# Attention units followed by their transposes one unit later, weight decoding in smaller steps, an earlier load of x

## The chip, the core and the metric

One NeuronCore of a Trainium2 chip runs the kernel. The metric is the device time of one execution in microseconds (us). Engines: TensorE (PE, its weight loads PEld), VectorE (DVE), ScalarE (ACT), GpSimd (POOL), and SyncE (SP), which issues most of the transfers.

## The reference

Inputs are float32 q, k, v of shape 4 x 8 x 768 x 64 (batch, heads, positions, width), a 64 x 6 projection, and float64 weights of a feed-forward block. What is computed, cut to its core:

```python
q_bits = (einsum('bhsd,dk->bhsk', q, proj) > 0)        # six sign bits per position; k_bits alike
mask   = q_bucket[:, :, :, None] == k_bucket[:, :, None, :]
scores = where(mask, (q @ k.T) / 8, -1e9)
attn   = exp(scores - max); attn /= attn.sum(-1) + 1e-9
x      = (attn @ v), heads side by side                 # 4 x 768 x 512
h      = relu(x @ w_in)                                  # 512 -> 1024
conv   = three taps along the positions, per channel of h
out    = (h * sigmoid(conv)) @ w_out                     # 1024 -> 512
```

## The kernel before

**Attention.** Two heads of a batch are a pair; there are 16 pairs (`pi` 0 to 15). A pair has 12 units (`Unit`), one for 128 queries of one head, so there are 192 units. One loop over `i` (L452) writes the program, and the order of its calls is the order of the instructions on every engine; no scheduler moves anything. Step `i` issues for unit `u = units[i]` the four score products (`products`, L276, PE, tile s in PSUM), the row maximum with the copy to SBUF (`maximum`, L284, DVE, tile e), the exponential (L291, ACT) and, for the unit before, the sum's end and its reciprocal (L295, L298, DVE) and the scaling (`normalise`, L299, POOL). For unit `w = units[i - LAG]` it issues six transposes (`transposes`, L304, PE, tile t in PSUM) and their copy (`to_sbuf`, L311, ACT, tile at). After every fourth `w` the product with v follows one step later (`values`, L319, 24 matmuls, called V below), and at the step after that its copy out of PSUM (L324, DVE, tile x) and a store to DRAM (xd, L325).

Three PSUM buffers under the tag "S" are taken in turn by s, t and the pair's hash. So the transposes of step `i` take the buffer that the scores of unit `i - 1` leave free, once DVE has done the maximum of unit `i - 1`. The value products and later the hidden layer take turns in two buffers under the tag "M". e has `EB` buffers.

**The next pair.** In steps k = 1 to 7 of each pair, `prepare` splits the next pair's q and k, tile R, into a high and a low part (L194 and L199 on POOL, for each of two heads), computes the hash (L209, L212, L214), and moves the parts by transfers of SP's queue. R has one buffer: its next load (L181) waits for those transfers.

**Weights.** 16 blocks of 128 x 512 float64 weights are fetched (L164, one each six steps) and decoded to two float32 parts. A block takes four DVE instructions (L94, L96, L101, L103), two on ACT (L86, L135) and three on POOL (L89, L138, L139). `split_weights` is a generator; from step `DECODE` on, every second step takes one piece of it:

```python
if i >= DECODE and i % 2 == 0:
    next(weights_todo, None)
```

**x of batch 0** is loaded from DRAM at the start of pair `X0` (L371, four transfers) and split on POOL by one instruction each third step (L379, L381).

**Feed-forward.** At `i == n` (192) `feed_forward` starts. Each of its steps has 12 matmuls of the hidden layer (L342, tile h under the tag "M"), Relu and first tap on ACT (L347, L349), two taps on DVE (L351), Sigmoid on ACT (L354), a product on DVE (L355), a split (L360 ACT, L361 POOL), and the output product (L391). Its first steps are interleaved with the last units' transposes.

Of the kernel before, what the change touches and what calls it, by code (L numbers as in the profile page):

```python
# [7 lines left out]
F32 = mybir.dt.float32  # L8
F32R = mybir.dt.float32r
# [3 lines left out]
ALU = mybir.AluOpType  # L13
# [4 lines left out]
P = 128  # L18
# [9 lines left out]
MASKED = -8.0e9  # L28
F32_MAX = 2.0 ** 127 * (2.0 - 2.0 ** -23)
F64_MIN = 2.0 ** -15  # L30
LAG, EB = 3, 5
FLAG = 3
BURST = 4
PREP = 1
PREP_N = 6
DECODE = 14
FETCH = 6
X0 = 8
WC = 512


# [1 line left out]
def lsh_attention_conv_ffn(ctx, tc, qk, v, hw, w_in, conv_w, w_out, consts, ident_in, out):  # L43
    nc = tc.nc
    PSUM = bass.MemoryType.PSUM
    cp = ctx.enter_context(tc.tile_pool(name="const", bufs=1))
# [19 lines left out]
    weights = {}  # L66
# [6 lines left out]
    class Decode:  # L73
# [17 lines left out]
        def upper(self):  # L91

            V, up, low = nc.vector, self.up, self.low
            V.tensor_scalar(low, low, 3, 0x3FFFFFFF, ALU.logical_shift_left, ALU.bitwise_and)  # L94
            yield
            V.scalar_tensor_tensor(up, self.hi, -0x40000000, low, ALU.bitwise_and, ALU.bitwise_or)  # L96
            yield

        def lower(self):
            V, up, low = nc.vector, self.up, self.low  # L100
            V.tensor_scalar(low, up, -0x800000, None, ALU.bitwise_and)  # L101
            yield
            V.scalar_tensor_tensor(self.lowf, self.lo, 2.0 ** -52, self.lowf, ALU.mult, ALU.mult)  # L103
            yield

    def split_weights():

        todo, ends = [], None

        def ahead():
            if fetched:
                raw, name = fetched.pop(0)
                todo.append(Decode(raw, WC, name))
                todo[-1].size()

        ahead()
        ahead()  # L120
        yield
        for d in todo:
            d.clamp()
        yield
        while todo:
            d = todo.pop(0)
            ahead()
            yield from d.upper()
            if ends:
                ends()  # L130
            if len(todo) == 2:
                todo[-1].clamp()
            yield from d.lower()
            blk = weights[d.name] = cp.tile([P, 2, WC], F32R, tag=f"w{d.name}", name=f"w{d.name}")
            nc.scalar.copy(blk[:, 0, :], d.upf)  # L135

            def ends(d=d, blk=blk):
                nc.gpsimd.tensor_tensor(d.upf, d.upf, blk[:, 0, :].bitcast(F32), ALU.subtract)  # L138
                nc.gpsimd.tensor_tensor(blk[:, 1, :], d.upf, d.lowf, ALU.add)  # L139

        ends()

    def decode_taps(raw):
        d = Decode(raw, NFC * 3, "cw")
        d.size()
        yield
        d.clamp()
        yield
        yield from d.upper()
        yield from d.lower()  # L150
        nc.vector.tensor_tensor(cw.rearrange("p f k -> p (f k)"), d.upf, d.lowf, ALU.add)


# [2 lines left out]
    blocks += [(w_out[f * P:(f + 1) * P], f"o{f}") for f in range(NFC)]  # L156
    fetched, taps = [], []
    weights_todo = split_weights()

    def fetch(n):  # L160
# [287 lines left out]
    next(first)  # L448
    pairs[1].load()
    n, tail, x0 = len(units), None, None  # L450
    outs, av, splits = [], None, iter(())
    for i in range(n + LAG + 1):  # L452
        u = units[i] if i < n else None
        w = units[i - LAG] if LAG <= i < n + LAG else None
        prev = units[i - 1] if 1 <= i <= n else None
        pi, k = divmod(i, 2 * NCK)
        burst = w and w.tq == QB // P - 1 and w.h == 1
        if u:
            u.products()
            u.maximum(prev)  # L460
        elif prev:
            prev.total()
        for o in outs:
            o()
        outs = []
        if w:
            w.transposes()
            w.to_sbuf()
        if u:
            u.exponential()  # L470
        if prev:
            prev.normalise()
        if i in (0, 2):
            next(first, None)
        if u and k == PREP and pi + 1 < len(pairs):
            prep[0] = pairs[pi + 1].prepare()
        next(prep[0], None)
        if av:
            outs.append(values(*av))
            av = None  # L480
        if burst:
            av = w.pair, w.qb, w.pair.at
        if u and k == PREP + PREP_N and pi + 1 < len(pairs):
            pairs[pi + 1].load_v()
            if pi + 2 < len(pairs):
                pairs[pi + 2].load()
        if i == 3:
            taps.append(decode_taps(cwr))
        for g in taps:
            next(g, None)  # L490
        if i % FETCH == FETCH - 1:
            fetch(1)
        if i >= DECODE and i % 2 == 0:
            next(weights_todo, None)
        if pi == X0 and k == 0:
            x0 = load_x(0)
            splits = split_x(x0)
        if x0 and k % 3 == 2:
            next(splits, None)
        if i == n:  # L500
            tail = feed_forward(x0)
        if tail:
            next(tail)
# [47 lines left out]
```

## Time and profile before

| | |
|---|---|
| time, median of 3 runs | 767.1 us (765.78 to 767.71) |
| the profiled execution's own time | 765.89 us |
| its span (first to last instruction) | 764.1 us, mean granted clock 0.985 |
| PE busy | 711.3 us (93%) |
| DVE busy | 489.6 us (64%) |
| ACT busy | 486.2 us (64%) |
| POOL busy | 448.4 us (59%) |
| attention | from 7 to about 477 us |
| feed-forward | from about 477 us to the end |

Read the table with care for stages: in the feed-forward part PE has matmuls without a break, so what the change is worth is read from the attention part and from the place where the two meet. Times of DMA and engines overlap; a wait counts only where PE stands behind it.

### The profile page before, as it was taken

How to read it: one execution, taken by the hardware profiler on the slowest of the kernel's cores; microseconds unless marked ns; L12 is line 12 of the kernel's file. 1: busy time of each engine (PE TensorE's matmuls, PEld its weight loads, DVE VectorE, ACT ScalarE, POOL GpSimd, SP SyncE). 2: the span in 40 equal slices, each digit the busy share in tenths (PEclk: the TensorE clock that was granted, in tenths of full speed). 3: DMA queues.
4: the chain of work that ended last, by engine and by line, in shares of the span. 5: the costliest groups of instructions: out<-in, count | busy, mean ns of one | idle time of the engine just before them, and what ended most of it. 6: DMA issues, size and time to landing. Idle time of an engine off the chain costs nothing.

```text
span 764.1 us, 13725 instructions
## 1 busy us (share of the span) xinstructions
PE 711.3 (93%) x4552; PEld 579.4 (76%) x4552; DVE 489.6 (64%) x1303; ACT 486.2 (64%) x892; POOL 448.4 (59%) x422
## 2 busy tenths in 40 slices
PE   5999888899898888989999999889999999999997
PEld 3767666667677666677777777778989899899986
DVE  7656776676667657666666655357666756665553
ACT  5777767677677756777777777535454545545453
POOL 5775776877867779878766553145326524642222
PEclk8999999999999989999999999999999999999999
DMA  3767556557566744653655640201210121101011
GB/s 110 185 182 202 157 172 178 156 169 212 131 186 180 215 133 108 177 146 83 175 146 131 185 104 15 90 7 42 80 45 1 42 84 41 42 1 42 0 42 42
DMA packets 39575, 84.79 MB, mean 111 GB/s; under 512 B 6960, under 2 KB 14672, under 8 KB 39504
## 3 DMA queue, kind: packets, MB, share of 16 engines
q1 hardware_dynamic: 36912, 75.47, 35.8%
q10 hardware_dynamic: 2592, 8.44, 3.3%
q8 instruction: 37, 0.61, 0.3%
q14 instruction: 34, 0.28, 0.1%
HBM read 33.70 MB, written 12.58 MB: 61 GB/s over the span
## 4 chain that ended last, share of the span: by engine, by line
PE 66%; DVE 19%; DMA 5%; POOL 4%; issue 3%; ACT 2%; SPq 1%; DVEq 0%; POOLq 0%; ACTq 0%
PE o L391 17%; PE h L342 17%; PE v L319 15%; DVE e L284 10%; PE s L276 8%; PE t L304 7%; DMA R<-in_qk 3%; POOL e L299 2%; DMA k<-R 2%; DVE wli L103 1%; DVE wlo L103 1%; PE hash L209 1%; DVE st L298 1%; DVE st L288 1%; DVE st L295 1%
## 5 line engine op out<-in xcount | busy, mean ns | idle before, releaser
L284 DVE TENSOR_SCALAR_CACHE_REDUCE e<-s 128x768 f32<-128x768 f32 x192 | 182.9, 953 | 137.4 <-PE s L276 120.5
L299 POOL TENSOR_SCALAR e<-e,st 128x768 f32<-128x768 f32 x192 | 186.1, 971 | 114.8 <-DVE st L298 98.5
L311 ACT COPY at<-t 128x768 f32<-128x768 f32 x192 | 151.8, 791 | 103.7 <-PE t L304 103.5
L291 ACT ACTIVATE e<-e,st 128x768 f32<-128x768 f32 x192 | 180.4, 940 | 25.2 <-DVE st L298 21.5
L304 PE MATMUL t<-ident,e 128*128 128x128 f32 x1152 | 162.9, 278 | 33.4 <-DVE st L295 26.5
L304 PEld LDWEIGHTS t<-ident,e 128*128 128x128 f32 x1152 | 131.0, 142 | 62.1 <-POOL e L299 52.1
L361 POOL TENSOR_TENSOR g<-ht,g 128x384 fp32r<-128x384 f32 x64 | 69.7, 1088 | 170.5 <-ACT g L360 138.2
L351 DVE SCALAR_TENSOR_TENSOR ht<-ht,cw 128x384 f32<-128x384 f32 (+1 forms) x128 | 119.2, 931 | 73.6 <-ACT ht L349 71.0
L342 PE MATMUL h<-x,wi 128*128 128x386 f32 x768 | 147.7, 341 | 2.7 <-DVE x L324 2.7
L342 PEld LDWEIGHTS h<-x,wi 128*128 128x128 f32 x768 | 138.0, 190 | 8.9 <-DVE x L324 3.1
L391 PE MATMUL o<-wo,g 128*128 128x512 f32 x576 | 143.6, 394 | 0.0
L319 PE MATMUL v<-at,v 128*64 128x256 f32 x1152 | 137.8, 387 | 2.1 <-ACT at L311 2.1
L391 PEld LDWEIGHTS o<-wo,g 128*128 128x128 f32 x576 | 107.2, 188 | 20.5
L319 PEld LDWEIGHTS v<-at,v 128*64 128x64 f32 x1152 | 79.5, 138 | 52.9 <-issue 15.9
L276 PE MATMUL s<-K,Q 128*128 128x384 f32 x384 | 116.3, 384 | 1.5 <-POOL K L243 1.2
L276 PE MATMUL s<-k,q 96*128 96x384 f32 x384 | 99.8, 341 | 2.3 <-DVE e L284 2.1
L354 ACT ACTIVATE ht<-ht 128x384 f32<-128x384 f32 x64 | 33.6, 525 | 96.9 <-DVE ht L351 96.9
L276 PEld LDWEIGHTS s<-K,Q 128*128 128x128 f32 x384 | 58.6, 192 | 21.8 <-issue 18.9
L276 PEld LDWEIGHTS s<-k,q 96*128 96x128 f32 x384 | 70.9, 191 | 3.1 <-ACT q L256 3.1
L355 DVE TENSOR_TENSOR ht<-ht 128x384 f32<-128x384 f32 x64 | 47.5, 741 | 33.7 <-ACT ht L354 33.7
L347 ACT ACTIVATE ht<-h 128x386 f32<-128x386 f32 x64 | 31.6, 494 | 37.3 <-PE h L342 37.1
L199 POOL TENSOR_TENSOR R<-R,hi 128x768 fp32r<-128x768 f32 x30 | 54.8, 1828 | 0.0
(65 smaller groups left out, 512.2 us busy)
## 6 DMA issues: line engine op xcount, KB each, us to landing
R<-in_qk SPq DMA_DIRECT2D x15, 768.0 KB
K<-hi SPq DMA_DIRECT2D x60, 192.0 KB
v<-in_v SPq DMA_DIRECT2D x16, 384.0 KB
xd<-x SPq DMA_DIRECT2D x48, 128.0 KB
x<-xd SPq DMA_DIRECT2D x16, 384.0 KB
out<-osb SPq DMA_DIRECT2D x24, 256.0 KB
Q<-hi SPq DMA_DIRECT2D x30, 192.0 KB
q<-hi SPq DMA_DIRECT2D x30, 192.0 KB
```

The costliest lines, as they stand in the source:

```text
L199: nc.gpsimd.tensor_tensor(lo, R, hi.bitcast(F32), ALU.subtract)
L276: nc.tensor.matmul(self.sp[:, half, :HS], A[:, h, qs], C[:, h, half * HS:(half + 1) * HS], start=(kk == 0), stop=(kk == 1))
L284: nc.vector.tensor_scalar(self.e.rearrange("p (a b) -> p a b", a=2), self.sp[:, :, :HS], MASKED, None, ALU.max, ALU.max, accum_out=self.st ...
L291: nc.scalar.activation(self.e, self.e, AF.Exp, bias=self.st[:, 1:2], scale=SCALE, accum_out=self.st[:, 2:3])
L299: nc.gpsimd.tensor_scalar(self.e, self.e, self.st[:, 3:4], 0.0, ALU.mult, ALU.add)
L304: nc.tensor.transpose(self.tp[:, c // 3, c % 3 * P:(c % 3 + 1) * P], self.e[:, c * P:(c + 1) * P], ident)
L311: nc.scalar.copy(pr.at[self.h][:, :, :, self.tq * P:(self.tq + 1) * P], self.tp[:, :, :3 * P].rearrange("p j (c q) -> p j c q", c=3))
L319: nc.tensor.matmul(av[h * D:(h + 1) * D, :QB], pr.v[:, c, h, :], ats[h][:, c // 3, c % 3, :], start=(c == 0), stop=(c == NCK - 1), tile_po ...
L342: nc.tensor.matmul(hp[:, :HW], w, x[:, c0:c0 + HW], start=(n == 0), stop=(n == 3 * NCC - 1))
L351: nc.vector.scalar_tensor_tensor(t[:, a:z], ht[:, o + k - 1 + a:o + k - 1 + z], cw[:, f, k:k + 1], t[:, a:z], ALU.mult, ALU.add)
L361: nc.gpsimd.tensor_tensor(g[:, 1, :], t, g[:, 0, :].bitcast(F32), ALU.subtract)
L391: nc.tensor.matmul(op, l, r, start=(f == 0 and i == 0), stop=(f == NFC - 1 and i == 2))
```

## The change

Four things change. `LAG` goes from 3 to 4 and `EB` from 5 to 6: the transposes of a unit come four steps after its products, and e has six buffers. The decoding of a weight block is cut into eight pieces instead of four (a DVE instruction in every other one, the POOL instructions in pieces of their own), it starts at step 10 instead of 14, and three of four steps take a piece (`RATE` 0.75) instead of every second one. x of batch 0 is loaded at the start of pair 6 (the seventh) and split from pair 9 on, instead of both from pair 8 on. The last pair's last V is followed at once by its copy. The number of instructions on each engine stays as it was.

```diff
-LAG, EB = 3, 5
+LAG, EB = 4, 6
-DECODE = 14
+DECODE, RATE = 10, 0.75
-X0 = 8
+X0, X0_SPLIT = 6, 9
...
     def split_weights():
-        todo, ends = [], None
+        todo, ends = [], iter(())
...
+        def finish(d, blk):
+            nc.gpsimd.tensor_tensor(d.upf, d.upf, blk[:, 0, :].bitcast(F32), ALU.subtract)
+            yield
+            nc.gpsimd.tensor_tensor(blk[:, 1, :], d.upf, d.lowf, ALU.add)
+
-        ahead()
         ahead()
         yield
-        for d in todo:
-            d.clamp()
+        todo[-1].clamp()
         yield
         while todo:
             d = todo.pop(0)
-            ahead()
-            yield from d.upper()
-            if ends:
-                ends()
-            if len(todo) == 2:
-                todo[-1].clamp()
-            yield from d.lower()
-            blk = weights[d.name] = cp.tile([P, 2, WC], F32R, tag=f"w{d.name}", name=f"w{d.name}")
-            nc.scalar.copy(blk[:, 0, :], d.upf)
-
-            def ends(d=d, blk=blk):
-                nc.gpsimd.tensor_tensor(d.upf, d.upf, blk[:, 0, :].bitcast(F32), ALU.subtract)
-                nc.gpsimd.tensor_tensor(blk[:, 1, :], d.upf, d.lowf, ALU.add)
-
-        ends()
+            steps = [*d.upper(), *d.lower()]
+            for k, step in enumerate(steps):
+                step()
+                if k == 3:
+                    blk = weights[d.name] = cp.tile([P, 2, WC], F32R, tag=f"w{d.name}", name=f"w{d.name}")
+                    nc.scalar.copy(blk[:, 0, :], d.upf)
+                yield
+                if k < 2:
+                    next(ends, None)
+                elif k == 2:
+                    ahead()
+                elif todo:
+                    todo[-1].clamp()
+                yield
+            ends = finish(d, blk)
+
+        for _ in ends:
+            yield
...
         if av:
             outs.append(values(*av))
             av = None
+            if not w:
+                outs.pop()()
...
-        if i >= DECODE and i % 2 == 0:
-            next(weights_todo, None)
+        if i >= DECODE:
+            due += RATE
+            if due >= 1:
+                due -= 1
+                next(weights_todo, None)
...
-        if x0 and k % 3 == 2:
+        if pi >= X0_SPLIT and k % 3 == 2:
             next(splits, None)
```

**The order that it makes.** In the order before, V stands at the end of every step i with i mod 4 = 3; in the changed one, with i mod 4 = 0. Below, place 0 is a step with V at its end, and places 1, 2 and 3 are the steps after it. Before, the 64 DVE instructions of the decoding stand at place 1 (all 16 of L96 and all 16 of L103) and at place 3 (L94 and L101). In the changed order 16 stand at place 0, 22 at place 1 (six first, five second, five third and six fourth instructions of a block), none at place 2 and the others at place 3.

DVE before, around step 64 (place 1): e is the maximum's output, st a unit's row sums, x the copy of V's result v, wli a decoded block's lower part.

```order
L284 TENSOR_SCALAR e_1_2_0_2059,st_1_2_0_2058<-s_1_2_0_2053 128x768
L295 TENSOR_SCALAR st_1_1_1_2012<-st_1_1_1_2012 128x1
L288 TENSOR_SCALAR st_1_2_0_2058<-st_1_2_0_2058 128x1
L324 COPY x_0_2_2063<-v_0_2_2040 128x256
L298 RECIPROCAL st_1_1_1_2012<-st_1_1_1_2012 128x1
L103 SCALAR_TENSOR_TENSOR wli_1_1404<-rawi_1_1192,wli_1_1404 128x512
L284 TENSOR_SCALAR e_1_3_0_2093,st_1_3_0_2092<-s_1_3_0_2087 128x768
```

DVE changed, around the same step 64 (now place 0; lines moved: L288 is the maximum, L328 the copy, L101 the block's fourth instruction):

```order
L288 TENSOR_SCALAR e_1_2_0_2019,st_1_2_0_2018<-s_1_2_0_2013 128x768
L299 TENSOR_SCALAR st_1_1_1_1984<-st_1_1_1_1984 128x1
L292 TENSOR_SCALAR st_1_2_0_2018<-st_1_2_0_2018 128x1
L302 RECIPROCAL st_1_1_1_1984<-st_1_1_1_1984 128x1
L101 SCALAR_TENSOR_TENSOR wli_1_1694<-rawi_1_998,wli_1_1694 128x512
L288 TENSOR_SCALAR e_1_3_0_2067,st_1_3_0_2066<-s_1_3_0_2061 128x768
L299 TENSOR_SCALAR st_1_2_0_2018<-st_1_2_0_2018 128x1
L292 TENSOR_SCALAR st_1_3_0_2066<-st_1_3_0_2066 128x1
L328 COPY x_0_2_2071<-v_0_2_2045 128x256
```

The decoding instruction kept its step, but V and the copy of its result moved from before it to behind it.

DVE before, where attention ends and feed-forward begins (x_3_1 is the copy of the last V but one, ht the hidden layer's tile):

```order
L295 TENSOR_SCALAR st_3_5_1_5811<-st_3_5_1_5811 128x1
L324 COPY x_3_1_5843<-v_3_1_5829 128x256
L298 RECIPROCAL st_3_5_1_5811<-st_3_5_1_5811 128x1
L351 SCALAR_TENSOR_TENSOR ht_0_0_5878<-ht_0_0_5878,cw 128x383
L351 SCALAR_TENSOR_TENSOR ht_0_0_5878<-ht_0_0_5878,cw 128x384
L355 TENSOR_TENSOR ht_0_0_5878<-ht_0_0_5878 128x384
```

DVE changed, at the same place:

```order
L299 TENSOR_SCALAR st_3_5_1_5803<-st_3_5_1_5803 128x1
L302 RECIPROCAL st_3_5_1_5803<-st_3_5_1_5803 128x1
L355 SCALAR_TENSOR_TENSOR ht_0_0_5867<-ht_0_0_5867,cw 128x383
L355 SCALAR_TENSOR_TENSOR ht_0_0_5867<-ht_0_0_5867,cw 128x384
L359 TENSOR_TENSOR ht_0_0_5867<-ht_0_0_5867 128x384
L328 COPY x_3_1_5878<-v_3_1_5832 128x256
L355 SCALAR_TENSOR_TENSOR ht_0_1_5902<-ht_0_1_5902,cw 128x383
```

The copy moved behind the three DVE instructions of the hidden layer's first step. On PE the changed order there is: transposes of unit 188, V of units 184 to 187, 12 matmuls of h_0_0, transposes of unit 189, 12 matmuls of h_0_1; the last of these take the "M" buffer that this V had. Before, the V of units 184 to 187 stood one step ahead of the first h, and the last V of all behind the third; now the last V stands behind the fourth h and the first output product.

## Rows read from the trace of the kernel before

**Rows 1.** Stretches: us, then busy us (and count) of PE, PEld, DVE, ACT, POOL; clock; DMA

```profile
80.00:120.00 40.00, 35.44 (x264) 27.54 (x264) 28.17 (x94) 28.63 (x53) 30.83 (x31) 1.00 0.53 149
...
440.00:480.00 40.00, 39.79 (x299) 31.55 (x293) 22.13 (x90) 30.02 (x55) 18.11 (x19) 1.00 0.25 67
```

**Rows 2.** Waits of PE and PEld, 40 to 360 us: us in total, times, longest

```profile
PE t L304 <- DVE st L295: 25.0, 29, 1.8
PE t L304 <- POOL e L299: 5.3, 4, 2.9
...
PEld t L304 <- POOL e L299: 43.9, 45, 3.2
```

**Rows 3.** Timeline, step 40 (place 1): start, us, engine, line, tiles, [idle before]

```profile
108.19 1.86 POOL L199 TENSOR_TENSOR R<-R,hi 128x768 fp32r<-128x768 f32 x1
...
108.44 2.15 DVE L103 SCALAR_TENSOR_TENSOR wli<-rawi,wli 128x512 f32<-128x512 uint32 x1
...
110.00 1.37 POOL L299 TENSOR_SCALAR e<-e,st 128x768 f32<-128x768 f32 x1
...
110.52 0.94 DVE L284 TENSOR_SCALAR_CACHE_REDUCE e<-s 128x768 f32<-128x768 f32 x1
...
111.61 0.85 PE L304 MATMUL t<-ident,e 128*128 128x128 f32 x6 [1.77 <-DVE st L295]
```

**Rows 4.** Timeline, step 44 (place 1)

```profile
119.07 0.68 DVE L96 SCALAR_TENSOR_TENSOR wui<-rawi,wli 128x512 int32<-128x512 int32 x1
...
120.76 0.85 PE L304 MATMUL t<-ident,e 128*128 128x128 f32 x6 [0.51 <-DVE st L295]
```

**Rows 5.** Line 103, first eight blocks: shortest, median, longest in ns

```profile
L103 DVE SCALAR_TENSOR_TENSOR wli<-rawi,wli x8: 672/1782/2150, 68.7 to 207.4; 128x512 f32<-128x512 uint32 x8
```

**Rows 6.** Chain that ended last, two V three apart: start, us, what

```profile
403.46 2.74 PE v L319 x24
...
430.43 2.74 PE v L319 x24
```

**Rows 7.** Timeline, pair 8, after the first split of x

```profile
262.17 1.82 POOL L381 TENSOR_TENSOR x<-x 128x768 fp32r<-128x768 f32 x1
...
269.43 0.87 PE L304 MATMUL t<-ident,e 128*128 128x128 f32 x6 [2.93 <-POOL e L299]
...
272.10 1.54 PE L304 MATMUL t<-ident,e 128*128 128x128 f32 x6 [0.81 <-POOL e L299]
...
276.13 3.40 PE L319 MATMUL v<-at,v 128*64 128x256 f32 x24
```

**Rows 8.** Timeline, where attention ends

```profile
479.88 0.48 ACT L347 ACTIVATE ht<-h 128x386 f32<-128x386 f32 x1
...
480.14 2.39 PE L342 MATMUL h<-x,wi 128*128 128x386 f32 x12
...
482.99 0.56 DVE L355 TENSOR_TENSOR ht<-ht 128x384 f32<-128x384 f32 x1 [0.59 <-ACT ht L354]
...
487.98 4.42 PE L319 MATMUL v<-at,v 128*64 128x256 f32 x22 [2.08 <-ACT at L311]
...
499.04 0.42 DVE L324 COPY x<-v 128x256 f32<-128x256 f32 x1
...
499.51 3.80 PE L342 MATMUL h<-x,wi 128*128 128x386 f32 x12 [2.66 <-DVE x L324]
```

**Rows 9.** Timeline, the last copy ahead of a V, without decoding beside it

```profile
392.32 0.79 ACT L311 COPY at<-t 128x768 f32<-128x768 f32 x1
...
393.39 2.36 PEld L319 LDWEIGHTS v<-at,v 128*64 128x64 f32 x24 [0.17 <-issue]
```

**Rows 10.** Timeline, first split of R in pairs 3 and 4

```profile
102.35 0.83 POOL L194 TENSOR_SCALAR hi<-R 128x768 fp32r<-128x768 f32 x1 [1.11 <-PE t L304]
...
133.14 0.83 POOL L194 TENSOR_SCALAR hi<-R 128x768 fp32r<-128x768 f32 x1 [2.01 <-DVE st L298]
```

**Rows 11.** Timeline, the first transposes of all

```profile
15.62 1.48 PE L304 MATMUL t<-ident,e 128*128 128x128 f32 x6
```

More of the change, by code (lines that the diff above doesn't have):

```diff
@@ L93, in upper @@
             V, up, low = nc.vector, self.up, self.low
[L94 to L97, printed above, removed]
+            return (lambda: V.tensor_scalar(low, low, 3, 0x3FFFFFFF, ALU.logical_shift_left, ALU.bitwise_and),
+                    lambda: V.scalar_tensor_tensor(up, self.hi, -0x40000000, low, ALU.bitwise_and,
+                                                   ALU.bitwise_or))
         def lower(self):
             V, up, low = nc.vector, self.up, self.low
[L101 to L104, printed above, removed]
+            return (lambda: V.tensor_scalar(low, up, -0x800000, None, ALU.bitwise_and),
+                    lambda: V.scalar_tensor_tensor(self.lowf, self.lo, 2.0 ** -52, self.lowf, ALU.mult, ALU.mult))
     def split_weights():
-        todo, ends = [], None
+        todo, ends = [], iter(())
         def ahead():
@@ L148, in decode_taps @@
         yield
-        yield from d.upper()
-        yield from d.lower()
+        for step in (*d.upper(), *d.lower()):
+            step()
+            yield
         nc.vector.tensor_tensor(cw.rearrange("p f k -> p (f k)"), d.upf, d.lowf, ALU.add)
@@ L450, in lsh_attention_conv_ffn @@
     n, tail, x0 = len(units), None, None
-    outs, av, splits = [], None, iter(())
+    outs, av, splits, due = [], None, iter(()), 0
     for i in range(n + LAG + 1):
```

## The prediction

> **What bounds the kernel now.** I read the stretches of 40 us first. The reader is to see two rates in the attention part: while weights are decoded PE runs 264 matmuls in 40 us and is busy 35.4 us; late, when decoding is over, 299 and 39.8 us [rows 1]. The work of a pair is the same in both, so PE is the bound, and what slows it is beside the decoding. Second, PE's waits: between 40 and 360 us nearly all idle time of PE stands before the transposes, 25.0 us in 29 waits put down to DVE and 5.3 us in 4 to POOL; PEld's waits there name POOL's scaling, 43.9 us [rows 2]. Third, the timeline of single waits, since a transposition needs two things: the scaled e of its own unit, and the PSUM buffer that DVE frees with the maximum of the unit before.
>
> In step 40 the decoding's L103 follows the copy of V's result and holds DVE for 2.15 us; only then does the next maximum start (110.52 us). It ends at 111.46, and the transposes start at 111.61 after 1.77 us of idleness. POOL's scaling ended at 111.37 [rows 3]. So both had come within a tenth of a microsecond, the maximum last. With a short instruction, L96 of 0.68 us, the same place costs 0.51 us [rows 4]. At place 3 the same kind of instruction delays a maximum that is needed only after V, and V lasts 2.74 us [rows 6]: no wait of PE follows there.
>
> Without such waits three V, one pair, take 430.43 - 403.46 = 27.0 us [rows 6].
>
> **The change part by part**, against the profiled execution's 765.9 us.
>
> *Lead and buffers.* With four units of lead a unit's scaling has one more unit's PE time, so POOL's lateness of 0.1 to 1 us behind many of PEld's waits [rows 2] stops mattering. The maximum that frees the PSUM buffer is that of the unit before, whatever the lead. The lead alone therefore takes little from the 25.0 us; it shifts V by one step against the decoding. Six buffers keep e as before: unit i takes the buffer of unit i - 6, whose transposes stand in step i - 2; before it was i - 5, and i - 2 too. Cost 0. The Trainium skill speaks against the lead, too: by "Perfetto Trace Analysis", section "Identifying Performance Opportunities", a bubble that repeats can mean too few buffers of SBUF or PSUM for the next tile, and here the PSUM buffers stay three. The waits [rows 3, 4] agree with it, and by that rule the lead would give 0 of the 25.0 us; my sum takes that term from the place of the decoding alone.
>
> *Decoding.* All 64 DVE instructions remain. At place 1 there were 32 and are 22. Price of one there: 0.51 us for a short one [rows 4], 1.77 for a long L103 [rows 3]; L103 itself lasts between 0.67 and 2.15 [rows 5]. I take 0.5 for each of the 22, the value of the short one: 11.0 us in place of 25.0, **-14.0**. Why short: the long L103 ran beside POOL's L199, 108.19 to 110.05 [rows 3], which the steps k = 3 and 7 issue; V now stands behind k = 4 and 8, so L199 should be over before place 1 begins. Bounds: if first and third steps (11) cost nothing, 5.5 us; if each costs the mean of before, 25.0/29 = 0.86, 19.0. So -19.5 to -6.0. Instructions at place 0 and 3 I cost at nothing: V hides them. If that cover failed, each would cost 0.5 too. Spread until step 185, they also reach the last pairs, where there was no decoding; the 22 include those.
>
> On ACT the copy and the Abs of a block, always at place 3 before, stand 11 times at place 1. There they push back the copy that V waits for. Its margin without decoding is 0.28 us: it ends at 393.11, V's loads start at 393.39 [rows 9]. A push of some 0.6 us leaves 0.3 to 0.4, but where PE waits for DVE anyway it is hidden: **+2** (0 to 4).
>
> POOL's three decoding instructions are issued in three different steps instead of two or three at once: nothing on PE, helped by the lead.
>
> *x of batch 0.* In pair 8 its splitting (L381, 1.82 us) delays POOL so that two transpositions wait 2.93 and 0.81 us; this one and the next V then run longer, 1.54 for 0.87 and 3.40 for 2.74 us [rows 7, 6], 1.3 us together, and I put as much on the groups between them. These 6.3 us go: **-6.3** (-7 to -3). In pairs 9 and 10 the eight splitting instructions come one per third step, behind a lead of four. The rest of PE's waits for POOL, 5.3 - 3.7 = 1.6 us [rows 2, 7], goes with the lead: **-1.6**. The four loads of x move on SP's queue ahead of the transfers of pair 6's first split, where weights are still fetched. Not seen before; they delay the second split (its buffer must be read first), which queues the scalings behind it on POOL. Below: nothing, the lead covers it; above: the 2.93 us of [rows 7]. I take **+1**.
>
> *Handover to feed-forward.* Before, PE waits 2.08 us for the last copy and 2.66 us for the last V's copy by DVE, and what follows runs longer: V 4.42 us for 22 matmuls against 2.74 for 24 [rows 6], the hidden step 3.80 against 2.39: 2.08 + 1.9 + 2.66 + 1.4 = 8.0 us [rows 8]. In the changed order the last V stands two groups of matmuls later, so most of that goes. But a new wait comes: the second hidden step needs the "M" buffer of the V before, whose copy now stands behind L355 of the first hidden step. The chain from the first Relu to that copy's end is 482.99 + 0.56 + 0.42 - 479.88 = 4.1 us; the second hidden step, which could begin at 480.14, waits to 483.97, 3.8 us [rows 8]. I add 1.7 for running longer afterwards, as the two waits above did on average, and 0.7 for the last copy, which is still a little late. 6.2 for 8.0: **-1.8** (-8 without the new wait, +1 if the slow stretch doubles).
>
> *Start.* The first transposes fall into a gap of PE and last 1.48 us [rows 11]; now they come one unit later, where PE has no gap: **+1** (0 to 1.5).
>
> Sum: -14.0 + 2 - 6.3 - 1.6 + 1 - 1.8 + 1 = -19.7, so 746.2 for an execution like the profiled one. The median of the runs shown is 1.2 us above it: **747.4 us**.
>
> **The rivals.**
>
> *The lead gives more.* The waits of place 1 fall to 5.5 us (lower bound), ACT costs nothing, nothing runs longer at the handover: 747.4 - 5.5 - 2 - 1.7 = 738.2. For it: late pairs run at 39.8 of 40 us [rows 1].
>
> *The long instruction stays long.* The six fourth steps at place 1 meet a POOL instruction as in [rows 3]: 6 x (1.77 - 0.51) = 7.6 more, 755.0. For it: the median of the first eight is 1.78 us [rows 5], nearer the long end. Against: L199 is over earlier. L103 ran until 110.59 beside an L199 that ended at 110.05 [rows 3]. By the Trainium skill, "SBUF", section "Who interferes with whom", a DVE instruction with two SBUF inputs and a GpSimd instruction that reads SBUF block each other for the whole instruction. These two agree with it; by it, every decoding instruction with two inputs that meets one of POOL's would be long.
>
> *Every decoding instruction costs the same wherever it stands* (the change does not do what its places say): the 25.0 us stay, 761.4. Against: no wait follows place 3.
>
> *The circle of R becomes the bound.* R's next load waits for transfers that wait for POOL and SP. From split to split it took 133.14 - 102.35 = 30.8 us, and POOL then idled 2.01 us at its end [rows 10]; a pair could take 27.0. While weights are fetched (pairs 1 to 7) pairs could not get shorter; then 7 of the 11 pairs that decoded before gain nothing of the decoding's term: 747.4 + 14.0 x 7/11 = 756.3. Against: part of the 30.8 us is paced by PE's own steps, which get shorter, and V's new place leaves three V instead of two between the hash's bits and the next split.
>
> *Slower than before: POOL falls behind.* Decoding and splitting now meet in pairs 9 and 10, and decoding goes on in 12 to 14. If each of these five gets a wait as in [rows 7], 6.3 us with its slow stretch, it is 747.4 + 31.5 = 778.9; from the fourth such wait on (772.6) the change is slower. For: POOL is busy 30.8 of 40 us, and works in order [rows 1]. Against: the lead, and fewer of its instructions per step.
>
> **How the numbers follow.** Forecast 0.50 (742 to 752); more gain 0.19; long instruction 0.12; circle of R 0.07; all places alike 0.08; slower 0.04. Time: the likeliest, 747.4. The range, 738 to 758, leaves out the places-alike and the slower case (0.12) and what of the second lies under 738 (0.08). A measurement here can tell 0.3% (2.3 us) from no change. Faster by more than that in all cases but the last and a rest of misfits: 0.93; same 0.03; slower 0.04.
>
> **What would show it.** Right: PE's waits "t <- DVE" of about 11 us in some 22 places, each after a decoding instruction at place 1; no long wait near pair 8; late pairs as long as early ones, near 28 us; one wait of about 3.5 us before the second hidden step, its releaser the copy of a V. Wrong: waits of transposes for POOL that are not small, hash waiting for R by more than 1 us in most of the pairs, waits at places 0 or 3, V waiting for copies by more than 4 us, or the feed-forward part longer than before.

## The result and the profile after

The changed kernel takes 739.95 us (median of 4 runs, 738.06 to 742.1), the kernel before 766.44 us beside it (764.02 to 767.71): a ratio of 0.966, 95% interval 0.962 to 0.970. The forecast was 747.4 us, a ratio of 0.974, with a range of 738 to 758. So the direction and the range held, and the gain was larger than forecast. The profiled execution of the changed kernel took 738.06 us, its span is 736.2 us (764.1 before), its mean granted clock 0.992.

Lines have moved by about four: transposes are now L308, scores L280, the maximum L288, the scaling L303, at L315, V L323, the copy of its result L328, h L346. The decoding's four DVE instructions are L94, L95, L100, L101.

Stretches of 40 us of the changed kernel (columns as in [rows 1]):

```profile
80.00:120.00 40.00, 38.82 (x290) 30.75 (x292) 29.70 (x107) 31.93 (x58) 29.95 (x31) 1.00 0.66 181
280.00:320.00 40.00, 38.93 (x288) 30.25 (x286) 30.00 (x99) 30.35 (x55) 38.46 (x36) 1.00 0.64 171
400.00:440.00 40.00, 39.04 (x293) 30.86 (x291) 28.89 (x102) 30.76 (x56) 27.27 (x27) 1.00 0.37 98
```

The two rates of [rows 1] have become one: 290 matmuls early, 293 late, where there were 264 and 299. Pairs 1 to 14 last 27.0 to 28.7 us; before it was 28.6 to 30.7 while weights were decoded, 34.8 in pair 8 and 27.0 to 27.6 at the end. In 280 to 320, where x is split, POOL is busy 38.46 of 40 us, and PE still runs 288 matmuls.

Waits of PE and PEld between 40 and 360 us in the changed kernel, as in [rows 2]:

```profile
PE t L308 <- DVE st L299: 9.0, 18, 1.0
PE hash L213 <- DMA R<-in_qk: 1.5, 3, 0.6
...
PEld t L308 <- POOL e L303: 14.4, 20, 1.3
```

The 25.0 us of waits for DVE are 9.0, the 5.3 for POOL are gone, and what PEld waits for POOL fell from 43.9 to 14.4. In the whole execution the waits for DVE are 11.3 us in 23. All but one stand behind a decoding instruction at place 1. The timeline of the changed kernel at a step of place 1 and at step 64, place 0:

```profile
134.06 0.67 DVE L101 SCALAR_TENSOR_TENSOR wli<-rawi,wli 128x512 f32<-128x512 uint32 x1
134.65 0.95 DVE L288 TENSOR_SCALAR_CACHE_REDUCE e<-s 128x768 f32<-128x768 f32 x1
135.75 0.84 PE L308 MATMUL t<-ident,e 128*128 128x128 f32 x6 [0.52 <-DVE st L299]
...
156.88 2.81 PE L323 MATMUL v<-at,v 128*64 128x256 f32 x24
157.57 1.84 DVE L101 SCALAR_TENSOR_TENSOR wli<-rawi,wli 128x512 f32<-128x512 uint32 x1
160.71 0.96 DVE L288 TENSOR_SCALAR_CACHE_REDUCE e<-s 128x768 f32<-128x768 f32 x1 [1.30 <-PE s L280]
```

At place 1 even a short L101 of 0.67 us costs PE 0.52. At place 0 an L101 of 1.84 us costs nothing: it runs under V, and the next maximum then waits 1.30 us for PE, not PE for it. No instruction at place 0 (up to 2.19 us long) or at place 3 has a wait behind it. (By the trace the 64 decoding instructions stand 22 at place 1 and 21 each at places 0 and 3; the 16 given above for place 0 is a miscount that enters no sum.)

The handover in the changed kernel, to be read beside [rows 8]:

```profile
458.33 0.56 DVE L359 TENSOR_TENSOR ht<-ht 128x384 f32<-128x384 f32 x1 [0.59 <-ACT ht L358]
458.81 0.42 DVE L328 COPY x<-v 128x256 f32<-128x256 f32 x1
459.28 2.39 PE L346 MATMUL h<-x,wi 128*128 128x386 f32 x12 [3.50 <-DVE x L328]
...
470.52 2.80 PE L323 MATMUL v<-at,v 128*64 128x256 f32 x22 [0.65 <-ACT at L315]
473.25 2.37 PE L346 MATMUL h<-x,wi 128*128 128x386 f32 x12
```

The new wait is there, 3.50 us for 3.8 forecast, its releaser the copy behind the hidden step's DVE work. The last copy costs 0.65 us for 0.7 forecast. In this execution nothing runs longer behind them: 2.39, 2.80 and 2.37 us, where V had 4.42 and h 3.80 before [rows 8]. That is not the rule. The same wait of 3.5 us stands in eight of the runs below, and in all eight the h behind it took longer, 3.16 to 4.23 us. In the run "place 1 left free", with the granted clock of the stretch, which is the lower level (1.2 GHz):

```profile
456.96 4.23 PE L346 MATMUL h<-x,wi 128*128 128x386 f32 x12 [3.50 <-DVE x L328]
```

```profile
456.00:462.00 6.00, 5.04 (x17) 4.95 (x18) 0.89 (x2) 1.35 (x3) 0.00 (x0) 0.50 0.06 22
```

The profiled execution of the change is the fastest of its four; whether the other three were spared this too, no trace shows.

### The profile page after: what moved, and what is told of

Read it like the earlier page. It is cut to its first block, busy times and chain, and to the rows that moved or that the text cites. A ratio compares the mean times of both kernels' runs of the same rounds, so it can differ in the third digit from the quotient of the medians.

```text
span 736.2 us, 13666 instructions
## 1 busy us (share of the span) xinstructions
PE 704.8 (96%) x4552; PEld 580.5 (79%) x4552; DVE 498.2 (68%) x1303; ACT 485.9 (66%) x892; POOL 450.9 (61%) x422
## 4 chain that ended last, share of the span: by engine, by line
PE 73%; DVE 10%; DMA 5%; POOL 4%; ACT 3%; issue 3%; SPq 2%; POOLq 0%; DVEq 0%; ACTq 0%
PE o L395 18%; PE h L346 18%; PE v L323 15%; PE s L280 11%; PE t L308 10%; DVE e L288 5%; DMA R<-in_qk 3%; DMA k<-R 2%; POOL e L303 2%; PE hash L213 2%; ACT at L315 1%; SPq L201 1%; ACT e L295 1%; POOL R L203 1%; DVE x L328 1%
## 5 line engine op out<-in xcount | busy, mean ns | idle before, releaser
L288 DVE TENSOR_SCALAR_CACHE_REDUCE e<-s 128x768 f32<-128x768 f32 x192 | 182.9, 953 | 91.9 <-PE s L280 84.9
L303 POOL TENSOR_SCALAR e<-e,st 128x768 f32<-128x768 f32 x192 | 186.8, 976 | 90.1 <-DVE st L302 75.4
L315 ACT COPY at<-t 128x768 f32<-128x768 f32 x192 | 152.2, 793 | 89.8 <-PE t L308 89.7
L308 PE MATMUL t<-ident,e 128*128 128x128 f32 x1152 | 159.7, 275 | 11.4 <-DVE st L299 11.3
L308 PEld LDWEIGHTS t<-ident,e 128*128 128x128 f32 x1152 | 130.3, 141 | 33.6 <-POOL e L303 16.5
L346 PE MATMUL h<-x,wi 128*128 128x386 f32 x768 | 146.0, 339 | 3.5 <-DVE x L328 3.5
L346 PEld LDWEIGHTS h<-x,wi 128*128 128x128 f32 x768 | 136.4, 188 | 9.5 <-DVE x L328 3.7
L323 PE MATMUL v<-at,v 128*64 128x256 f32 x1152 | 136.5, 383 | 0.7 <-ACT at L315 0.6
L280 PE MATMUL s<-K,Q 128*128 128x384 f32 x384 | 116.7, 385 | 1.8 <-POOL K L247 1.2
L323 PEld LDWEIGHTS v<-at,v 128*64 128x64 f32 x1152 | 82.7, 137 | 41.0 <-issue 8.1
L280 PE MATMUL s<-k,q 96*128 96x384 f32 x384 | 99.5, 340 | 2.3 <-DVE e L288 1.8
L280 PEld LDWEIGHTS s<-K,Q 128*128 128x128 f32 x384 | 58.5, 192 | 31.8 <-issue 17.8
L280 PEld LDWEIGHTS s<-k,q 96*128 96x128 f32 x384 | 70.8, 191 | 3.1 <-ACT q L260 3.1
```

Of the source, the lines that this page charges most:

```text
L280: nc.tensor.matmul(self.sp[:, half, :HS], A[:, h, qs], C[:, h, half * HS:(half + 1) * HS], start=(kk == 0), stop=(kk == 1))
L288: nc.vector.tensor_scalar(self.e.rearrange("p (a b) -> p a b", a=2), self.sp[:, :, :HS], MASKED, None, ALU.max, ALU.max, accum_out=self.st ...
L303: nc.gpsimd.tensor_scalar(self.e, self.e, self.st[:, 3:4], 0.0, ALU.mult, ALU.add)
L308: nc.tensor.transpose(self.tp[:, c // 3, c % 3 * P:(c % 3 + 1) * P], self.e[:, c * P:(c + 1) * P], ident)
L315: nc.scalar.copy(pr.at[self.h][:, :, :, self.tq * P:(self.tq + 1) * P], self.tp[:, :, :3 * P].rearrange("p j (c q) -> p j c q", c=3))
L323: nc.tensor.matmul(av[h * D:(h + 1) * D, :QB], pr.v[:, c, h, :], ats[h][:, c // 3, c % 3, :], start=(c == 0), stop=(c == NCK - 1), tile_po ...
```

## Experiments

Two theories stood against each other at first. **Place**: what a decoding instruction on DVE costs is set by where it stands against V. **Lead and rate**: the gain comes from POOL's slack or from smaller, rarer pieces. All times are medians; each ratio is against the kernel before, run beside it. "The change" is the changed kernel.

| run | us | ratio | 95% interval |
|---|---|---|---|
| the change | 739.95 | 0.966 | 0.962 to 0.970 |
| lead alone | 757.75 | 0.989 | 0.985 to 0.993 |
| lead, decoding at places 1 and 3 | 755.28 | 0.986 | 0.982 to 0.991 |
| the change, place 1 left free | 737.7 | 0.963 | 0.959 to 0.966 |
| the change without the lead | 760.06 | 0.991 | 0.988 to 0.994 |
| the change, copy first | 736.24 | 0.963 | 0.960 to 0.967 |
| the change, x in pair 8 | 740.55 | 0.969 | 0.965 to 0.972 |
| the change, five e | 743.07 | 0.971 | 0.966 to 0.975 |
| lead, pieces spread, one a step | 753.62 | 0.985 | 0.980 to 0.990 |
| the same, two steps later | 761.38 | 0.995 | 0.992 to 0.997 |
| lead alone, two R | 749.6 | 0.980 | 0.977 to 0.983 |
| places 0 and 3, copy first | 733.67 | 0.959 | 0.956 to 0.963 |
| the same with two R | 724.66 | 0.948 | 0.945 to 0.951 |

### Lead alone

```diff
-LAG, EB = 3, 5
+LAG, EB = 4, 6
...
+            if not w:
+                outs.pop()()
```

> The kernel before with only the lead of four units, the six buffers and the earlier last copy; the decoding keeps its four steps a block, every second step, and x stays in pair 8. V shifts by one step, so the 64 DVE instructions of the decoding stand at places 0 and 2 instead of 1 and 3. Theory (the place decides): place 0 is covered by V; place 2 has no copy of V's result ahead of it, so it costs 0 to 0.25 us for each of 32. Waits of transposes for DVE 0 to 8 us (before: 25.0), time 738 to 750. Rival A (smaller steps and the lower rate brought the gain): the waits stay above 20 us, time 755 to 764. Rival B (only the lead's slack for POOL counts): PE's waits for POOL go, those for DVE stay at 25 us, time 752 to 758.

757.75 us. Waits of PE in this run, whole execution:

```profile
PE hash L209 <- DMA R<-in_qk: 9.4, 7, 2.1
PE t L304 <- POOL e L299: 5.0, 7, 1.3
...
PE t L304 <- DVE st L295: 0.9, 3, 0.5
```

The theory's waits came out as it said, 0.9 us instead of 26.5, and its time did not: the hash now waits 9.4 us for R. The pairs alternate, 27.9 and 31.4, 27.9 and 32.4 us. POOL's timeline in pair 3 of this run shows why:

```profile
103.55 1.28 POOL L138 TENSOR_TENSOR wui<-wui,wi 128x512 f32<-128x512 f32 x1
104.92 1.29 POOL L139 TENSOR_TENSOR wi<-wui,wli 128x512 fp32r<-128x512 f32 x1
106.28 0.95 POOL L89 TENSOR_SCALAR wli<-wli 128x512 f32<-128x512 f32 x1
...
110.78 0.58 POOL L214 TENSOR_SCALAR bits<-bits,cst 128x384 fp32r<-128x384 f32 x1
```

The three decoding instructions come in a row in the middle of the preparation, and the hash's bits (L214), begun on DVE at 103.4, leave POOL at 111.4. Their transfers and R's next load follow late. A block takes 8 steps, a pair 12, so every second pair is hit. This is the "circle of R", a rival that had been given 0.07 for the change itself.

The waits are not all of it. PE at pair 8 of this run, transposes and V, and the stretch that holds them:

```profile
270.49 0.87 PE L304 MATMUL t<-ident,e 128*128 128x128 f32 x6 [1.19 <-DVE e L284]
273.32 1.54 PE L304 MATMUL t<-ident,e 128*128 128x128 f32 x6 [1.27 <-POOL e L299]
...
277.36 3.80 PE L319 MATMUL v<-at,v 128*64 128x256 f32 x24
```

```profile
240.00:280.00 40.00, 35.67 (x235) 26.90 (x235) 26.94 (x87) 27.16 (x50) 33.06 (x31) 0.87 0.75 211
```

The granted clock of the stretch is 0.87: part of it ran at the lower level (1.2 GHz), behind the waits for R and for POOL. Between 132 and 280 us four stretches, 17.0 us together, have a granted clock of 0.50; three of them begin 0.4 to 1.6 us after the start of a hash that had waited 1.8 to 2.1 us for R. Added over pairs 1 to 14, PE's groups of matmuls are 13 us longer than in the change, and PE waits 8.3 us more: 21 us together, as much as these pairs are longer (408.9 and 387.6 us).

### Lead, decoding at places 1 and 3

```diff
-        if i >= DECODE and i % 2 == 0:
+        if i >= DECODE and i % 2 == 1:
```

> The same as the run with the lead alone, but decoding taken at odd steps, so that its DVE instructions stand at places 1 and 3 as in the kernel before, now behind a lead of four. Theory (the place decides, not the lead): the waits after place 1 come back, 32 of 0.5 to 0.9 us, 16 to 28 us, and the time is 10 to 20 us above the run with the lead alone, 753 to 764. Rival (a lead of four and six buffers absorb it): waits below 8 us, time within 3 us of the run with the lead alone.

755.28 us. Waits of PE in this run:

```profile
PE t L304 <- DVE st L295: 16.8, 30, 1.2
PE hash L209 <- DMA R<-in_qk: 7.4, 5, 2.2
```

As the theory says, the waits stand behind place 1 again, 29 of the 30, and moving the same instructions by one step turns 16.8 us into 0.9. The time did not follow: over pairs 1 to 14 PE waits 8.4 us more than in lead alone, but its groups of matmuls are 10.4 us shorter, with one stretch at the lower clock there instead of four. Waits for R stand in both runs.

At the same places the kernel before waits 26.5 us. Here nearly every wait is 0.5 to 0.7 us; those of 1.8 us are gone. This is not the slack that the lead gives to POOL, as the timeline of this run shows (the first line is the scaling that the transposes of the last line need):

```profile
65.96 0.91 POOL L299 TENSOR_SCALAR e<-e,st 128x768 f32<-128x768 f32 x1
...
70.06 0.67 DVE L103 SCALAR_TENSOR_TENSOR wli<-rawi,wli 128x512 f32<-128x512 uint32 x1
...
70.64 0.95 DVE L284 TENSOR_SCALAR_CACHE_REDUCE e<-s 128x768 f32<-128x768 f32 x1
...
71.75 0.52 PE L304 MATMUL t<-ident,e 128*128 128x128 f32 x3 [0.50 <-DVE st L295]
```

The scaling had ended 4.9 us before, and an instruction of 0.67 us still costs PE 0.50, as in the kernel before [rows 4]. What is gone is long instructions: before, nine waits of 1.3 to 1.8 us, 14.7 us together, stood behind an L103 of 1.47 to 2.25 us, eight of them beside POOL's L199 [rows 3]. The lead moved place 1 by one step against L199. Here L103 takes 0.67 to 0.88 us but for two, neither of them beside L199.

### The change, place 1 left free

```diff
-            due += RATE
-            if due >= 1:
-                due -= 1
+            if i % 4 != 1:
```

> The changed kernel with the same rate, 0.75 pieces a step, but the step left free is the one at place 1 instead of that at place 2. Theory (the place decides): the 22 waits after place 1, 11 us together, go; those now at place 2 cost 0 to 0.25 us each, 0 to 5 us together. Waits of transposes for DVE 1 to 6 us, time 6 to 11 us less than the changed kernel: 729 to 735. Rival (DVE has too much to do in any two steps without a V): the 0.5 us stand at place 2 as they did at place 1, 10 to 12 us, time 737 to 743, no change.

737.7 us. The waits for DVE fell from 11.3 to 2.9 us, as expected; the hash's waits for R grew from 2.9 to 5.9. The intervals of this run and of the change overlap, so the gain of some 2 us is not shown by the times. V runs 2.2 us longer over pairs 1 to 14, four of them 3.3 us, and the h at the handover takes the 4.23 us shown above. So DVE's waits at place 1 were partly in front of other costs.

### The change without the lead

```diff
-LAG, EB = 4, 6
+LAG, EB = 3, 5
```

> The changed kernel with the lead of three units and five buffers of before; decoding and x as changed. V moves back by one step, so the DVE instructions of the decoding stand at places 0 (26), 1 (16) and 2 (22). Theory (place for DVE, lead for POOL): 16 waits of 0.5 to 0.9 us at place 1, 8 to 14 us, at place 2 0 to 5 us; waits for POOL come back, above all where x is split in pairs 9 and 10 (POOL is busy 38.5 of 40 us there in the changed kernel), 4 to 12 us; the old handover is 2.7 us dearer. Time 746 to 760. Rival (decoding in smaller steps and x from pair 9 bring the gain, the lead nothing): 738 to 744.

760.06 us, 20 us more than the change: the upper end of the expectation, and the rival falls. PE's waits:

```profile
PE t L308 <- DVE st L299: 18.3, 32, 1.3
PE t L308 <- POOL e L303: 9.3, 11, 1.6
```

Of the 18.3 us, 9.9 stand behind place 2, where the change has no instruction and the expectation had put 5 at most; the 21 waits at place 1 (21, not 16, stand there) are 7.9 us, 0.5 behind an instruction of 0.67 us and 0.24 behind one of 0.41, as in the change with its lead. The edit thus moves the decoding against V as well as taking the lead away; the 9.3 us for POOL, gone in the change, are what can be put down to the lead's slack.

So neither the lead nor the new decoding does it alone. Against the kernel before beside them, the lead with the old decoding gives 8.4 us, the new decoding without the lead 6.1, and both together 26.5.

### The change, copy first

```diff
-            if not w:
+            if not u:
                 outs.pop()()
```

> The changed kernel, with the copy of the last V but one put ahead of the first hidden step's three DVE instructions. Theory: the wait of 3.5 us before the second hidden step is that of its buffer for this copy; it goes, the copy then stands 0.42 us in the way of the first tap, which nobody waits for. Time 2.5 to 4 us less than the changed kernel (739.95): 736 to 737.5. Rival: the hidden steps wait for Relu and taps anyway and the wait moves behind them: 739 to 741.

736.24 us. The wait of 3.50 us is gone and nothing has taken its place but 0.9 us at the last V; from the start of the last pair to the end it is 311.2 us instead of 313.9. The theory holds in the trace; the intervals of the two ratios overlap.

### The change, x in pair 8

```diff
-X0, X0_SPLIT = 6, 9
+X0, X0_SPLIT = 8, 8
```

> The changed kernel with x of batch 0 loaded and split in pair 8 again, one splitting instruction in each third step. Theory: the splitting instructions that come right behind the load push the scalings back and, at the start of the pair, R's split; a lead of four takes half of it: 3 to 7 us more than the changed kernel, 743 to 747, with a pair 8 of 31 us or more (28.1 now). Rival (the lead and the spread decoding cover it): 739 to 741.5.

740.55 us, the rival. Pair 8 lasts 28.6 us, with one wait for POOL of 0.9. The earlier load of x and its later splitting are worth nothing that can be measured here. Where decoding came in bunches (lead alone) pair 8 still took 33.6 us, with a lead of four and x in the same place. So with the lead and the spread decoding the incident of [rows 7] is gone without the move of x. In the change without the lead, where x was moved, pair 8 takes 29.6 us: moving x and spreading the decoding are enough too. Moving x alone was not run.

### The change, five e

```diff
-LAG, EB = 4, 6
+LAG, EB = 4, 5
```

> The changed kernel with five buffers of e instead of six, the lead still four. Theory: unit i then takes the buffer of unit i - 5, whose transposes stand in step i - 1, ahead of unit i's own score products on PE; the maximum that writes e waits for those products anyway, so the sixth buffer is not needed: 738.5 to 741.5, no wait of DVE for transposes. Rival (buffers of e are what the lead lives on): DVE's maxima wait for transposes and PE's waits for DVE grow by 5 us or more: 745 and above.

743.07 us, between the two; the intervals of this run and of the change overlap. In the attention part the waits for DVE are 10.5 us, no more than with six, so the rival's mechanism is absent. Of the 5.6 us by which the span is longer, 3.6 lie behind the start of the last pair (317.5 and 313.9 us). There h takes 3.73 us behind the wait at the handover, 1.3 more than in the change's profile, as in runs with six buffers, and one output product waits 1.24 us for a copy of a result. Neither is a wait for e, so a cost of the fifth buffer is not shown.

### Lead, pieces spread, one a step

The change with these constants, so that x and the rate per block are those of the lead alone:

```diff
-DECODE, RATE = 10, 0.75
+DECODE, RATE = 14, 1
-X0, X0_SPLIT = 6, 9
+X0, X0_SPLIT = 8, 8
```

> The run with the lead alone (757.75), but the decoding in eight pieces a block, one each step from step 14, so that a block takes eight steps as there, its DVE instructions stand at the same places (0 and 2), and only POOL's and ACT's pieces come apart; x in pair 8. Theory (in that run POOL's three decoding instructions in a row, 3.5 us, held up the hash's bits in every second pair, and R's next load with it): the hash's waits for R fall from 9.4 us to below 4, the pairs no longer alternate between 28 and 31 us, time 741 to 749. Rival (what counts is the rate of 0.75 a step): 753 to 759.

753.62 us. The first half of the theory holds: the hash's waits for R fall to 1.7 us. But pairs 2 to 7 still alternate, between 28.2 and 30 us, and the time misses: two costs appear that the lead alone did not have. Waits for DVE are 10.1 us, 8.2 of them behind an instruction at place 2. One of them, in the timeline of this run:

```profile
89.99 1.27 POOL L117 TENSOR_TENSOR wui<-wui,wi 128x512 f32<-128x512 f32 x1
90.06 1.76 DVE L95 SCALAR_TENSOR_TENSOR wui<-rawi,wli 128x512 int32<-128x512 int32 x1
...
92.84 0.84 PE L308 MATMUL t<-ident,e 128*128 128x128 f32 x6 [1.34 <-DVE st L299]
```

L95 takes 0.67 us alone. Beside L117 it took 1.76 and ended 0.56 us after it. By the Trainium skill, "SBUF — State Buffer", section "Who interferes with whom", a DVE instruction with two SBUF inputs and a GpSimd instruction that reads SBUF shut each other out for a whole instruction; this row agrees. At place 2 four such long L95 cost 1.3 to 1.4 us each, the shorter instructions there 0.55 or less. And V runs longer, 4.7 us in all over pairs 1 to 14 (0.4 in the change):

```profile
82.27 0.62 ACT L132 CAST wi<-wui 128x512 fp32r<-128x512 f32 x1
82.78 0.81 ACT L315 COPY at<-t 128x768 f32<-128x768 f32 x1
...
83.14 3.29 PE L323 MATMUL v<-at,v 128*64 128x256 f32 x24
```

The block's copy on ACT stands ahead of the last copy that V needs, and V takes 3.29 us for 2.81. This is the push by ACT that the prediction had priced at 2 us. It exists, but not at the places of the change.

### The same, two steps later

```diff
-DECODE, RATE = 14, 1
+DECODE, RATE = 16, 1
```

> The run with the spread decoding at one piece a step (753.6), begun at step 16 instead of 14 and else the same. The DVE instructions stay at places 0 and 2, but change places: the masking and the multiplying ones with two inputs (first seen at up to 1.79 us, each long one costing PE 1.35 us at place 2) go to place 0, the two short ones with one input to place 2, as in the run with the lead alone. Theory (what costs at place 2 is what an instruction lasts over some 0.4 us; at place 0 its length is free): waits of transposes for DVE fall from 10.1 to below 4 us, time 742 to 748. Rival (the rate of one piece a step is what costs): no change, 751 to 756.

761.38 us, a plain miss: waits for DVE rose to 22.1 us. The timeline shows what the expectation had overlooked:

```profile
111.92 0.61 POOL L89 TENSOR_SCALAR wli<-wli 128x512 f32<-128x512 f32 x1
112.57 0.43 DVE L94 TENSOR_SCALAR wli<-wli 128x512 int32<-128x512 int32 x1 [1.49 <-POOL wli L89]
...
114.01 0.85 PE L308 MATMUL t<-ident,e 128*128 128x128 f32 x6 [1.51 <-DVE st L299]
```

L94 is short, but it needs POOL's clamp L89, which is issued one step ahead of it and waits in POOL's order. DVE stands still for 1.49 us, with the next maximum queued behind. Over the run DVE waits 22.7 us for the clamp, in 16 places. In the run before, it had waited for the clamp too, 21.7 us in 12 places, but at place 0: one of these, of 4.08 us, cost PE 1.73, the others nothing. A second part is 6.2 us behind six L100, five of which took 1.52 us beside POOL's L119 instead of 0.41. What costs at place 2 is the time until the instruction ends, its own wait included. Whether rate alone would cost is not settled by these two runs.

### Lead alone, two R

```diff
-            self.R = ring(wp, 1, [P, 2, S], F32R, "R", f"R{nm}")
+            self.R = ring(wp, 2, [P, 2, S], F32R, "R", f"R{nm}")
```

> The run with the lead alone (757.75), with two buffers for R; the decoding's bunches stay. Theory (the circle of R bound every second pair there, and what follows a late hash runs longer): the hash's waits for R go (below 1.5 us), and with them the long running behind them, time 739 to 748. Rival (the bunches themselves delay the scalings, R is only late along with them): the waits become waits of transposes for POOL, time 752 to 758.

749.6 us, between theory and rival. The hash's waits for R have left the list of PE's longer waits, and the time falls by 8; the waits of transposes for POOL rise from 5.0 to 7.1 us. So the circle of R did bound the lead alone, and the bunches on POOL cost something beside it.

### Places 0 and 3

The copy first, and the decoding's DVE pieces at places 0 and 3 alone:

```diff
             due += RATE
-            if due >= 1:
-                due -= 1
-                next(weights_todo, None)
+            for _ in range(2):
+                if due >= 1 and (taken % 2 or i % 4 in (0, 3)):
+                    due, taken = due - 1, taken + 1
+                    next(weights_todo, None)
```

> The changed kernel with the earlier copy (736.2), and the decoding's DVE instructions issued at places 0 and 3 alone, at the same mean rate; the pieces without one go anywhere, up to two pieces in a step. Theory (the 22 waits after place 1 are all that DVE costs): waits of transposes for DVE below 3 us instead of 11.5, R's waits may grow by up to 3 us, since pairs get shorter: 726 to 732. Rival (two or more decoding instructions in neighbouring steps make DVE late at any place, or ACT's copies of a block push V): 733 to 738.

733.67 us. The place theory's waits are met in full, 0.6 us for DVE, with 64 decoding instructions on DVE as ever; its time of 726 to 732 is not. The gain over the run "copy first", 2.6 us, is not clear of the noise (the intervals overlap), because R takes over. The hash's waits and the longest of them:

```profile
PE hash L213 <- DMA R<-in_qk: 7.9, 8, 2.5
```

```profile
121.13 0.39 SPq L185 DMA_DIRECT2D R<-in_qk  x1
...
127.75 1.51 PE L213 MATMUL hash<-R,hw_sb 128*32 128x384 f32 x8 [2.55 <-DMA R<-in_qk]
```

The load is issued at 121.13, when the transfers of the pair before have left the one buffer, and R is there 6.6 us later; pair 4 takes 30.7 us.

The same with a second buffer for R (the edit shown above):

> The run with places 0 and 3, with two buffers for R. Theory (with DVE's waits gone the circle of R is the next bound, 3 to 6 us of hash waits): those go, 1 to 6 us less than the run with places 0 and 3, 723 to 730. Rival (hash waits for the load's own time in SP's queue, not for the buffer): within 1 us of it.

724.66 us, 9 us less, and the intervals lie apart. Waits of PE, and a stretch of this run:

```profile
PE hash L213 <- DMA R<-in_qk: 1.3, 2, 0.8
...
PE t L308 <- DVE st L299: 1.2, 1, 1.2
```

```profile
200.00:240.00 40.00, 40.00 (x304) 31.22 (x301) 27.71 (x102) 30.94 (x56) 30.20 (x31) 1.00 0.67 194
```

PE is busy without a break in stretches where weights are decoded; pairs 1 to 14 last 26.5 to 27.9 us, six of them less than the 27.0 us that a pair took in the kernel before without any decoding [rows 6]. This version beats both kernels: 0.948 of the time before, 15 us less than the change. A second R in the change itself was not run.

## Why the prediction was right, and where not

The terms of the sum against the two profiled spans (764.1 and 736.2 us; the forecast of 746.2 for an execution like the profiled one stands against 738.06). Waits and lengths are added over the groups of matmuls of pairs 1 to 14; the start of pair 1 and what follows the start of pair 15 are corrected for the transposes and the V that the lead moves across those borders (0.6 + 2.74 us).

| term | forecast | measured |
|---|---|---|
| decoding at place 1 | -14.0 | -15.5 |
| ACT pushes V | +2 | 0 |
| x, and POOL's other waits | -7.9 | -5.5 waits, -3.4 long running |
| load of x in pair 6 | +1 | +0.3 |
| handover | -1.8 | -2.9 |
| start | +1 | +1.0 |
| not in the sum | 0 | -1.9 |
| sum | -19.7 | -27.9 |

**Right, by its own steps.** The waits after place 1: 22 of 0.5 us were forecast, 11.0 us; 22 between 40 and 440 us make 10.5. The even 0.5 is in part luck: eight cost 0.23 to 0.25 us, behind an instruction of 0.41 us, and three 0.9 to 1.0, behind one that lasted 1.07 to 1.18 beside POOL. That place 0 is covered by V is shown three ways: by the change (1.84 us, no wait), by lead alone (0.9 us) and by places 0 and 3 (0.6 us). The new wait at the handover and its cause are right, and removing its cause removed it.

**Mis-sized.** The 8 us that were missing are no one term. Costs that were put in did not come: ACT's push (2), most of the load's (0.7), and running longer behind the handover's waits (1.7, of which the table has 1.1). The last is luck of the one profiled execution: in the eight runs with the same wait, h took 1.5 us longer on average, near the 1.7. Gains were a little larger: 1.5 for the decoding, 1.0 for POOL; 1.9 us by which the pairs are shorter could be assigned to no wait. The rival "the lead gives more" (738.2) was nearer than the forecast, for two of its three reasons, that of the handover only in the profiled execution; its own first one, that waits at place 1 cost 5.5 us, is not what happened.

**A step that looks wrong and is not.** "The lead alone takes little from the 25.0 us": yet with the decoding at the same places the lead cut these waits from 26.5 to 16.8 us. The reading of [rows 3] stands all the same. An instruction of 0.67 us at place 1 costs 0.5 us with a lead of three and with one of four, though POOL's scaling came 0.1 us before the maximum in the one and 4.7 us before it in the rows shown of the other. What went is the long L103 beside L199, by the step by which the lead shifts place 1; the prediction had this under "Why short" and put it into the decoding's term. The Trainium skill's rule on repeating bubbles, "Perfetto Trace Analysis", section "Identifying Performance Opportunities", which spoke against the lead, names too few buffers as what they can mean; these went (0.9 us in lead alone) with three PSUM buffers as before.

**A wrong step behind a right number.** The 6.3 us of x were booked for moving it. Its waits are gone, but with x back in pair 8 the time is the same. There the lead and the spread pieces carry it. Moving x without them was not run, so no run shows the term for the reason that it was given.

**The rivals.** The long instruction did not stay long at place 1, as argued: there L101 takes 0.67 us. Long ones moved to place 0, where they are free. The circle of R was taken as unlikely, and it is not the bound of the change; but it is the next one. Every edit that removed DVE's waits without a second R ran into it (5.9, 7.9 and 9.4 us of hash waits).

## What to carry to other kernels

A small instruction on a busy engine costs by its place in the repeating order: under the longest piece of PE's work (V, 2.8 us here) instructions of up to 2.2 us were free, a step later the same instruction costs nearly its own duration. Look for all its operands' producers too, since a piece that waits for another engine holds up what is queued behind it. And when a wait is taken away, look at the shortest cycle of loads and buffers that remains: here the best places for the decoding were worth no gain clear of noise by themselves (2.6 us), and a second buffer behind them 9 us more.

## What the runs showed of the hardware that was not expected

What follows a wait of PE differs from execution to execution. The wait of 3.5 us at the handover stands in nine traces: in that of the change the granted clock stayed at 1.00 and h ran in 2.39 us, in the eight others h took 3.16 to 4.23 us and the clock was 0.62 to 0.76 over the 7 us from its start. In the run with places 1 and 3 a hash that had waited 2.22 us for R was followed by 7 us at a clock of 1.00, one that had waited 1.98 us by 7 us at 0.76.

In the run with spread pieces, begun at step 14, four single waits of 1.3 to 1.4 us had transposes of about 0.85 us behind them. In the lead alone, a wait of 1.27 us that came 2.8 us after one of 1.19 had transposes of 1.54 and a V of 3.80 us behind it, in a stretch whose granted clock was 0.87. In the kernel before, 2.08 us of waiting at the handover were followed by a V of 4.42 us [rows 8]. A forecast of "longer afterwards" for one execution is therefore uncertain by its whole size, and one profile without it does not show that it is gone.
